# Weight rounding on one engine, the second product by groups of d_ff, contiguous decays and a shared table set in a linear attention and MLP kernel

## The chip, the cores and the metric

The kernel runs on one core of a Trainium2 chip. The time is the device time of one execution in microseconds (us), and "span" is the length of the profiled execution. TensorE (PE) multiplies, VectorE (DVE) and GpSimd (POOL) do elementwise work, ScalarE (ACT) does activations and copies, and SyncE (SP) issues most transfers. The outputs of matmuls land in PSUM, the other tiles lie in SBUF.

## The reference

Gated linear attention (4 batches, 8 heads, 768 positions, head size 48) makes 3072 rows of 384 columns. An MLP with 2048 hidden columns follows.

```python
f = 1.0 / (1.0 + np.exp(-f_logit))
for t in range(S):
    state = f[:, :, t, :, None] * state + np.einsum('bhd,bhe->bhde', k[:, :, t], v[:, :, t])
    y[:, :, t] = np.einsum('bhd,bhde->bhe', q[:, :, t], state)
x = y.transpose(0, 2, 1, 3).reshape(B * S, H * D)     # 3072 x 384
h = x @ w_in                                          # 384 x 2048
sp = np.maximum(h, 0.0) + np.log1p(np.exp(-np.abs(h)))
return ((h * erf(sp)) @ w_out).astype(np.float32)     # 2048 x 384
```

The two weights arrive as float64, since the reference scales them by a float64 number. The kernel rounds them to float32 on the chip, by arithmetic on the high and low 32-bit words.

## The kernel before

It works on 8 blocks of 384 rows, each of three token tiles (chunks) of 128. In pass `it` TensorE does the first product of block `it` in four groups of four d_ff slices, the second product of block `it - 1`, and between them the attention of block `it + 1`. There is one more pass for the last second product. A pass has 48 matmuls for each product, and the program counts them as slots, at which it inserts other engines' work.

The weights come in 16 pieces, eight for each weight, 768 columns a partition in float32. The rounding alternates between three engines:

```python
nc.scalar.activation(out=dst, in_=high.bitcast(FP32), func=AF.Abs)
yield
nc.gpsimd.tensor_scalar(out=dst, in0=dst, scalar1=TINY, scalar2=None, op0=ALU.max)
yield
nc.vector.tensor_scalar(out=bits, in0=bits, ...)              # exponent and mantissa into place
nc.vector.scalar_tensor_tensor(out=bits, in0=high, ..., in1=bits, ...)
nc.vector.tensor_scalar(out=high, in0=bits, ...)              # the mask
nc.vector.scalar_tensor_tensor(out=low, in0=low, ..., in1=high, ...)
if i >= FIRST_PIECES:
    yield
(nc.vector if i < FIRST_PIECES else nc.gpsimd).tensor_tensor(
    out=dst, in0=low.bitcast(FP32), in1=dst, op=ALU.add)
```

The second product goes by token tile. Each tile's sum has a PSUM tile of its own (of a pool of two), and needs all 16 slices of d_ff before the next tile starts:

```python
# project(it - 1, [tt], whole) for tt in 0, 1, 2
ops = {tt: ps_moe.tile([P, 2, 512], FP32, name="ops", tag="moe") for tt in tts if ...}
for ft in fts:                        # 0 .. 15
    nc.tensor.matmul(of[tt], lhsT=gr["h"][:, ft % FG, ...], rhs=w_out_sb[:, ft, :], ...)
    if ft == n_ft - 1:
        nc.scalar.copy(out=osb[:], in_=of[tt])
        nc.sync.dma_start(out=out[r : r + P, :], in_=osb[:])
```

An activation runs on a group of 1536 columns: Exp, Ln, four Squares each followed by a product on VectorE, Tanh, and a last product on VectorE. The products of the first matrix are evicted by VectorE.

## Time and profile before

The kernel took 732.22 us (median of 4 runs, 726.86 to 732.51), with a profiled span of 725.4 us.

| | PE | DVE | ACT | POOL |
|---|---|---|---|---|
| busy us before | 644.3 | 507.3 | 525.2 | 163.3 |
| share of the span | 89% | 70% | 72% | 23% |

The page's slices of the kernel before, each digit the busy share in tenths of one of 40 equal stretches (18.1 us each); PEclk is the granted clock of TensorE in tenths:

```profile
PE   2658765649799999999999999999999999999795
DVE  2788998898857765677568776679568656765640
POOL 1545877740320131001311030004202100000000
PEclk9879889779999999999999999999999999999988
```

The reader is to see two regimes: until slice 9 (about 163 us) VectorE is at least as full as TensorE; from slice 12 (about 200 us) until near the end TensorE is full. GpSimd does most of its work in the first regime.

Two further views of before: the line of TensorE's order in which the first product begins (start, duration, engine, source line, operation, in brackets the idle time before it and who ended it), and TensorE's waits after 232 us (total, times, longest):

```profile
45.88 4.40 PE L425 MATMUL hps<-xT,w_in_sb 128*128 128x384 f32 x8 [3.30 <-ACT xT L369]
...
PE ops L452 <- DVE Hg L395: 4.2, 1, 4.2
PE ops L452 <- ACT osb L460: 0.6, 1, 0.6
```

The copy of the sums (osb) costs TensorE 0.6 us in the whole of the later passes.

### The profile page before, as it was taken

What the parts mean: (1) busy time and instruction counts of PE and PEld (TensorE: products, weight loads), DVE (VectorE), ACT (ScalarE), POOL (GpSimd) and SP (SyncE); (2) the same over time, 40 slices, a digit from 0 to 9 for tenths busy, and PEclk for the clock granted to TensorE, in tenths of its full rate; (3) what the DMA queues carried; (4) which work ended last, traced back from release to release, by engine and by line L of the source; (5) the groups of instructions that cost most, each with busy time, mean ns of one, the idle gap of its engine ahead of it and who ended that gap; (6) DMA issues with size and microseconds to landing.
All of it is one profiled execution on the core that took longest, in us unless ns stands there. A gap on an engine that the chain in (4) does not pass through costs nothing.

```text
span 725.4 us, 9143 instructions
## 1 busy us (share of the span) xinstructions
PE 644.3 (89%) x3729; PEld 394.8 (54%) x3729; DVE 507.3 (70%) x422; ACT 525.2 (72%) x455; POOL 163.3 (23%) x100
## 2 busy tenths in 40 slices
PE   2658765649799999999999999999999999999795
PEld 1535442326466666666666666566666665555453
DVE  2788998898857765677568776679568656765640
ACT  4345564439898788867998599869978886889830
POOL 1545877740320131001311030004202100000000
PEclk9879889779999999999999999999999999999988
DMA  9964244600034002410223003300310000000001
GB/s 212 253 135 121 52 113 119 152 1 1 0 79 85 1 1 44 99 21 1 44 44 77 0 11 78 77 1 1 72 29 0 1 23 12 1 11 11 12 0 37
DMA packets 112176, 36.88 MB, mean 51 GB/s; under 512 B 103936, under 2 KB 107008, under 8 KB 112128
## 3 DMA queue, kind: packets, MB, share of 16 engines
q1 hardware_dynamic: 108672, 36.18, 20.9%
q8 instruction: 31, 0.51, 0.3%
q10 hardware_dynamic: 3456, 0.05, 0.2%
q14 instruction: 17, 0.14, 0.1%
HBM read 31.46 MB, written 4.72 MB: 50 GB/s over the span
## 4 chain that ended last, share of the span: by engine, by line
PE 64%; DVE 14%; ACT 11%; issue 5%; POOL 3%; DMA 2%; SPq 0%; ACTq 0%; DVEq 0%; POOLq 0%
PE ops L452 30%; PE hps L425 24%; DVE e L155 4%; PE y L144 3%; ACT x L150 2%; PE sc L323 2%; PE ps_t L310 2%; PE ps_d L279 1%; DVE Hg L248 1%; ACT e L379 1%; DVE w_out_sb L241 1%; ACT yl L382 1%; DVE w_out_sb L245 1%; DVE qd L292 1%; ACT e L393 1%
## 5 line engine op out<-in xcount | busy, mean ns | idle before, releaser
L425 PE MATMUL hps<-xT,w_in_sb 128*128 128x384 f32 x768 | 271.7, 507 | 29.4 <-DVE Hg L433 26.0
L452 PE MATMUL ops<-w_out_sb,Hg 128*128 128x384 f32 x768 | 263.2, 496 | 8.7 <-DVE Hg L395 8.2
L155 DVE SCALAR_TENSOR_TENSOR e<-x,e 128x1536 f32<-128x1536 f32 x128 | 240.1, 1876 | 6.3 <-ACT x L150 1.1
L425 PEld LDWEIGHTS hps<-xT,w_in_sb 128*128 128x128 f32 x768 | 148.1, 197 | 133.3 <-DVE Hg L433 24.2
L150 ACT ACTIVATE x<-yl,serf_bias 128x1536 f32<-128x1536 f32 x128 | 195.8, 1566 | 26.3 <-DVE e L155 25.3
L452 PEld LDWEIGHTS ops<-w_out_sb,Hg 128*128 128x128 f32 x768 | 144.8, 193 | 107.7 <-DVE Hg L395 9.4
L297 POOL TENSOR_TENSOR kd<-kn,dm 128x384 f32<-128x384 f32 x24 | 33.1, 1379 | 335.9 <-ACT dm L288 159.6
L395 DVE TENSOR_TENSOR Hg<-Hg,e 128x1536 f32<-128x1536 f32 x32 | 60.6, 1893 | 52.5 <-ACT e L393 52.3
L433 DVE COPY Hg<-hps 128x768 f32<-128x768 f32 x64 | 61.1, 955 | 35.5 <-PE hps L425 35.1
L292 DVE TENSOR_TENSOR qd<-qn,dp 128x384 f32<-128x384 f32 x24 | 23.1, 964 | 67.4 <-ACT dp L284 67.4
L393 ACT ACTIVATE e<-e 128x1536 f32<-128x1536 f32 x32 | 47.5, 1483 | 20.0 <-DVE e L155 18.4
L379 ACT ACTIVATE e<-Hg 128x1536 f32<-128x1536 f32 x32 | 47.4, 1480 | 16.0 <-DVE Hg L433 15.7
L382 ACT ACTIVATE yl<-e 128x1536 f32<-128x1536 f32 x32 | 47.5, 1484 | 0.3
L358 POOL TENSOR_TENSOR Mbd<-Sn,Tall 48x192 f32<-48x192 f32 x32 | 30.6, 956 | 61.5 <-DVE Sn L355 60.3
L144 PE MATMUL y<-A,vt 128*32 128x128 f32 x768 | 39.1, 296 | 5.8 <-DVE A L328 4.0
L382 ACT ACT_TABLE_LOAD x31 | 39.8, 1283 | 1.8 <-ACT dm L288 1.3
L144 PEld LDWEIGHTS y<-A,vt 128*32 128x32 f32 x768 | 29.7, 115 | 19.2 <-issue 11.8
L328 DVE TENSOR_TENSOR A<-sc,mask 128x1024 f32<-128x1024 f32 x24 | 29.3, 1219 | 10.2 <-PE sc L323 10.0
L284 ACT ACTIVATE dp<-ps_d 128x384 f32<-128x384 f32 x24 | 20.6, 859 | 18.0 <-PE ps_d L279 16.4
L144 PE MATMUL y<-qT,Mbd 128*32 128x128 f32 x480 | 33.1, 290 | 0.0
L323 PEld LDWEIGHTS sc<-qT,kT 48*128 48x128 f32 x384 | 23.7, 190 | 16.2 <-issue 12.5
L279 PE MATMUL ps_d<-lt,tri 128*128 128x384 f32 x48 | 21.4, 530 | 10.9 <-ACT lt L274 10.9
(59 smaller groups left out, 489.1 us busy)
## 6 DMA issues: line engine op xcount, KB each, us to landing
Hg<-in_moe_w_in_dram SPq DMA_DIRECT2D x8, 768.0 KB, 5.9
Hg<-in_moe_w_out_dram SPq DMA_DIRECT2D x8, 768.0 KB, 4.4
lt<-in_f_logit_dram SPq DMA_DIRECT2D x24, 192.0 KB, 3.7
qn<-in_q_dram SPq DMA_DIRECT2D x24, 192.0 KB, 3.8
kn<-in_k_dram SPq DMA_DIRECT2D x24, 192.0 KB, 3.6
vt<-in_v_dram SPq DMA_DIRECT2D x24, 192.0 KB, 3.7
out_dram<-osb SPq DMA_DIRECT2D x24, 192.0 KB, 2.0
Tall<-dp ACTq DMA_DIRECT2D x24, 2.0 KB, 1.9
```

The lines of the kernel that those rows point to most:

```text
L144: nc.tensor.matmul(y[M * i : M * (i + 1), kt, :], lhsT=terms[n][0], rhs=terms[n][1], start=(n == 0), stop=(n == len(terms) - 1), skip_grou ...
L150: nc.scalar.activation(out=dst[:], in_=y[:], func=AF.Square, bias=serf_bias[:, i : i + 1], scale=SERF_K)
L155: nc.vector.scalar_tensor_tensor(out=e[:], in0=x[:], scalar=SERF_AB[i][1], in1=e[:], op0=ALU.add, op1=ALU.mult)
L297: nc.gpsimd.tensor_tensor(out=kds[g % 2][:, :, 0:D], in0=kns[g % NQ][:].rearrange("t (h d) -> t h d", d=D), in1=dm[:].rearrange("t (h d) - ...
L323: nc.tensor.matmul(sc[:, r, a, :], lhsT=kT[rows(r), a, :], rhs=qT[rows(r), a, :], start=True, stop=True,)
L379: nc.scalar.activation(out=e[:], in_=h, func=AF.Exp)
L382: nc.scalar.activation(out=y[:], in_=e[:], func=AF.Ln, scale=SERF_C, bias=1.0)
L393: nc.scalar.activation(out=e[:], in_=e[:], func=AF.Tanh)
L395: nc.vector.tensor_tensor(out=h, in0=h, in1=e[:], op=ALU.mult)
L425: nc.tensor.matmul(hps[:, j, 0:TB], lhsT=w_in_sb[:, kt, ft * P : (ft + 1) * P], rhs=xTs[blk][:, kt, :], start=(kt == 0), stop=(kt == n_k - 1),
L433: nc.vector.tensor_copy(out=gr["h"][:, 2 * u : 2 * u + 2, :], in_=hps[:, :, 0:TB])
L452: nc.tensor.matmul(of[tt], lhsT=gr["h"][:, ft % FG, tt * P : (tt + 1) * P], rhs=w_out_sb[:, ft, :], start=(ft == 0), stop=(ft == n_ft - 1),)
```

## The change

The intent is to free TensorE from the rounding of the weights, which holds VectorE and GpSimd until 155 us, and to shorten the start and the tail. The main parts of the diff, cut:

```diff
@@ round_piece: all of it on VectorE, one instruction a step; words in halves of like counts
-        nc.gpsimd.tensor_scalar(out=dst, in0=dst, scalar1=TINY, scalar2=None, op0=ALU.max)
+        nc.vector.tensor_scalar(
+            out=halves(dst), in0=halves(dst), scalar1=TINY, scalar2=None, op0=ALU.max
+        )
...
-        (nc.vector if i < FIRST_PIECES else nc.gpsimd).tensor_tensor(
-            out=dst, in0=low.bitcast(FP32), in1=dst, op=ALU.add
-        )
+        nc.vector.tensor_tensor(out=dst, in0=low.bitcast(FP32), in1=dst, op=ALU.add)
@@ the raw words wait in w_out, in group buffers and in three spares
+            where = ["w", "w", "w", "w", 4, 5, 6, 3][i]
...
+            where = [4, 5, 6, "w", "w", "s0", "s1", "s2"][i - n_pieces]
@@ hidden: evictions of blocks 0 and 1 on ScalarE (and their kT copies)
+                        if blk < 2:
+                            nc.scalar.copy(out=to, in_=hps[:, :, 0:TB])
+                        else:
+                            nc.vector.tensor_copy(out=to, in_=hps[:, :, 0:TB])
@@ project: by groups of d_ff, three sums open at once in two PSUM tiles
+        ops = {tt: ps_moe.tile([P, 2, 512], FP32, name="ops", tag="moe")
+               for tt in range(0, CPB, 2)}
+        of = [ops[tt - tt % 2][:, tt % 2, 0:d_model] for tt in range(CPB)]
+        for gi in range(n_g):
+            for tt in range(CPB):
+                for j in range(FG):
...
                     if ft == n_ft - 1:
+                        osb = spares[0][:, ...]
+                        nc.scalar.copy(out=osb, in_=of[tt])
@@ one table set for Exp and Ln, loaded by hand
+    def use_exp_ln():
+        if sets[0] == EXP_LN:
+            return
+        sets[0] = EXP_LN
+        nc.scalar.add_instruction(mybir.InstLoadActFuncSet(act_func_set_id=EXP_LN, ...))
@@ stage_d: contiguous decays, their last row loaded in four parts on SyncE's queue
-        nc.scalar.dma_start(out=Tall[:, g, :], in_=dp[P - 1 : P].rearrange(...))
+        for a in range(HP):
+            nc.sync.dma_start(out=Tall[:, g, a : a + 1], in_=dp[P - 1 : P, ...])
@@ start: logits by chunk, k and v partly on ScalarE's queue
-        prepare(0, 0, CPB)
-        prepare_log(0, 0, CPB)
+        prepare(0, 0, 1)
+        prepare(0, 1, 2)
```

## The prediction

> **What bounds the kernel now.** I first read the page's forty slices: TensorE is 9 tenths busy in nearly all slices from the 12th on, at full clock, and ragged before. Then I read the busy time of each engine in four stretches, cut where TensorE's order changes: block 0's first product (46 to 120 us), the first third of the next pass (120 to 156), the rest of that pass (156 to 232) and one whole later pass (232 to 309).
>
> ```profile
> core 0: us, PE busy (x) PEld busy (x) DVE busy (x) ACT busy (x) POOL busy (x), PEclk, DMA share, GB/s
> ...
> 46.00:120.00 74.00, 55.95 (x384) 34.55 (x384) 65.76 (x59) 42.50 (x43) 49.66 (x24) 0.89 0.39 98
> 120.00:156.00 36.00, 16.37 (x58) 8.72 (x58) 32.79 (x28) 14.84 (x13) 24.81 (x11) 0.75 0.33 88
> 156.00:232.00 76.00, 71.07 (x404) 43.32 (x405) 59.65 (x46) 67.17 (x57) 11.55 (x8) 0.94 0.15 33
> 232.00:309.00 77.00, 76.42 (x469) 47.33 (x468) 51.14 (x41) 61.43 (x53) 11.91 (x8) 1.00 0.21 43
> ```
>
> From 232 us on TensorE is full; VectorE (51 of 77) and ScalarE (61 of 77) have slack. A pass is 96 matmuls, each two records of 0.3225 us (32 records took 10.32 us in the chain), 61.9 us, and about 15 us of attention: 76.8 us, which is the distance between equal places of the chain (235.2 to 312 to 389 us). Nothing in the change can shorten a full pass. What can be won lies before 232 us, where VectorE is busy 89% (65.76 of 74) and 91% (32.79 of 36) of the time, and in the tail. The waits of TensorE between 46 and 236 us name the same engine:
>
> ```profile
> PE hps L425 <- DVE Hg L433: 24.4, 4, 9.4
> PE ps_t L310 <- DVE qd L292: 6.7, 2, 6.1
> PE ps_t L310 <- DVE Sn L355: 5.6, 2, 5.3
> PE ops L452 <- DVE Hg L395: 4.0, 1, 4.0
> ```
>
> The evictions of the first product (L433) stand in VectorE's order behind the rounding of the weights. The rounding itself is stretched, as two groups of 46 to 156 us and two single instructions of the same line show:
>
> ```profile
> L241 DVE TENSOR_SCALAR w_out_sb<-w_out_sb 128x768 uint32<-128x768 uint32 x8 | 10.6, 1330 | 4.0 <-POOL w_out_sb L239 4.0
> L239 POOL TENSOR_SCALAR w_out_sb<-w_out_sb 128x768 f32<-128x768 f32 x8 | 23.7, 2974 | 0.0
> ...
> 93.88 2.22 DVE L241 TENSOR_SCALAR w_out_sb<-w_out_sb 128x768 uint32<-128x768 uint32 x1
> 105.31 0.54 DVE L241 TENSOR_SCALAR w_out_sb<-w_out_sb 128x768 uint32<-128x768 uint32 x1
> ```
>
> The same instruction took 2.22 us beside a GpSimd maximum and 0.54 us alone; its mean is 1.33 us.
>
> The tail: TensorE ran out once, for the last block's activations.
>
> ```profile
> 689.09 23.41 PE L452 MATMUL ops<-w_out_sb,Hg 128*128 128x384 f32 x64 [4.17 <-DVE Hg L395]
> ```
>
> **What the Trainium skill says.** "SBUF — State Buffer", § Who interferes with whom: a VectorE instruction in a two-port mode and a GpSimd instruction exclude each other for a whole instruction, and one with two SBUF inputs contends with GpSimd's reads. The trace agrees: 0.54 against 2.22 us. "VectorE: DVE Perf Modes", § The perf-mode tier table: in fp32 a tensor_scalar between SBUF tensors goes at 2x, a tensor_tensor at 1x; § Mode 2×_2P asks for outermost counts that are even, or equal. The trace agrees: the mask L248 takes 601 ns for w_out and 959 ns for w_in, whose two operands have unlike outer counts, and the diff's halves give them like ones. "ScalarE: Activation LUTs", § Table sets, puts Exp and Ln in one set, Tanh with Exp in another; § What ACT_TABLE_LOAD costs gives 1283 ns, which is the trace's mean, and a drain that the trace does not show (a load at 5.87 us, its activation at 7.17).
>
> **The change, part by part.**
>
> *Rounding.* Per piece, before, VectorE did four instructions for most pieces, GpSimd the maximum and the sum. Now VectorE does six. Uncontended: three at one source, 0.68 us (w_in) or 0.56 (w_out), and three with two sources at 0.96: 4.9 and 4.6 us. Sixteen pieces are 8 x 4.9 + 8 x 4.6 = 76 us, against 72 us that the before-trace's rounding groups on VectorE sum to, stretched. So VectorE takes over 74 us of GpSimd's work for 4 us of its own, and the round trips end.
>
> *Moved off VectorE.* The evictions of blocks 0 and 1, 16 x 0.95 = 15 us, and six copies of kT, 4 us, go to ScalarE (about 0.78 us for 768 columns, from 0.475 for 384 and 0.576 for 512). Onto VectorE: three kd products of block 0, 2.6 us, and six maxima of the logits, 6 x 0.77, which lie mostly later.
>
> *Start.* Logits are loaded and prepared by chunk, with the table loaded ahead: before, three loads of 1.28 us stood on the first chain, which waited to 5.9 us for all three chunks. Contiguous decays make Exp cost 0.53 us instead of 0.86. The first product started at 45.9 us; I estimate 35, as the first chunk's scan (10.9 us) may come 3 to 4 us earlier, chunks can follow each 6 us (the y of the first two stood at 22.2 and 28.5), and the third's slip to 39.6 and its copy's to 45.4 lay in waits on rounding. DMA was 93% busy until 46 us, so not much more.
>
> *First product of block 0.* In the new order VectorE has until the eighth w_in piece: six pieces 29.4, attention 3 x (0.85 + 1.22 + 0.70) + one kT and one logit maximum 1.5 = 9.8, two activation steps 3.5: 43 us. ScalarE has about 37.
>
> *To the end of rounding,* which now falls in the next pass: eight pieces 36.8, 15 activation steps and 4 products at 1.75 = 33.3, attention 8.3 + 2.2: 81 us. ScalarE in that pass: four groups x (3 x 1.48 + 4 x 1.57 + 2 x 1.28) = 53, eight evictions 6.2, seven Abs 6.4, attention 6.4, logits 3.6: 76 us. Both are near full and each waits for the other in order; in the stretch 156 to 232 the busier reached 88%. Taking 92% for the first and 90% for this: 35 + 47 + 90 = 172 us; the contiguous qd may give back some 2, so 170.
>
> *Second product by groups.* Only the last group of matmuls needs the last piece, and it is slot 72 of 96. So the pass ends at 170 + 24 x 0.645 + about 4 of attention = 189 us, against 232. Before, token tile 0 needed all sixteen slices of w_out and all four activated groups at slot 48.
>
> *Later passes* stay full. New in them: the three sums hold both PSUM tiles, so the last group's first product waits for ScalarE's copy of tile 1, issued only four matmuls (2.6 us) before; ScalarE may be two activations of 1.5 us behind. Estimate 0 to 1.5 us a pass, 4 us in all.
>
> *Tail.* The last block's fourth group is made at slots 48 to 63 instead of 72 to 83, and activation steps come each third slot: the waits of 4.2 and 1.05 us go, 5 us.
>
> Sum: 725.4 - (232 - 189) + 4 - 5 = 681 us of span; the profiled run measured 727.1 for a span of 725.4, so 682 us.
>
> **Rivals.** *TensorE full at once:* with 35 us of start, 46 for block 0's pass (48 matmuls 31 us and 15) and full passes, the second ends at 158 and the time is 650. VectorE's 124 us of sums before slot 72 speak against it. *ScalarE becomes the bound:* it gets 16 evictions, and in the second pass has 76 us against VectorE's 81; if the two alternate at 75%, rounding ends near 190 us and the time is near 702. For it: the activation chain alternates between them; against: 25 fewer table loads in the whole program order (70 against 95 before), worth 32 us of ScalarE. *The copy of the sums stalls every pass:* 3 us x 7 gives 698. Against: ScalarE idles 16 us a pass. *Start bound by DMA anyway:* the same bytes must come, so nothing is won before 46 us, and the time is 692.
>
> **Range and chances.** The rivals lie at 650, 692, 698 and 702; none of the milder ones comes back to 717 (2% below 732), and two would have to add up. Range 658 to 702. Faster 0.94, same 0.05, slower 0.01.
>
> **What would show it.** L241's counterpart should take 0.55 to 0.7 us, the mask 0.6 in both weights. First product at 35 us; VectorE busy about 90% until near 170; passes full from 189 on, 77 us apart. A wait of TensorE on ScalarE's copy of the sums beyond 1.5 us a pass, evictions late on ScalarE before 190 us, or DMA landing after its Abs is due, would make it wrong upward; VectorE ending rounding before 160 us, downward.

## The result, and the profile after

The changed kernel took 700.87 us (median of 4 runs, 698.70 to 703.94). The ratio is 0.9592 (95% interval 0.9531 to 0.9652): it is faster by 4.1%. Ratios here are the mean time of one kernel's fast runs over that of the kernel before in the same rounds, so not quite the ratio of the medians quoted. The profiled run took 698.7 us for a span of 697.0.

Source lines have moved: the first product is L476 (was L425), the second L509 (L452), the copy of the sums L518 (L460), the last product of an activation L442 (L395).

The page's slices of the kernel after (17.4 us each):

```profile
PE   3779997859999989999999989999899999999697
DVE  3779899889776675886667684675657864688410
POOL 0022101000112100011010110012001200000000
PEclk9799999989999999999999999999999999999799
```

TensorE reaches nines at the fourth slice, dips at the seventh to ninth, and is full from the tenth; GpSimd is nearly idle (66.2 us busy against 163.3). But in the right half TensorE's row has eights and a six, where before had nines and one seven, and PEclk has a seven near the end.

Windows of the kernel after, with the columns of the prediction's first fence (busy us and instructions for PE, PEld, DVE, ACT, POOL, then clock, DMA share, GB/s):

```profile
39.00:92.00 53.00, 50.14 (x388) 31.40 (x389) 46.38 (x57) 35.64 (x44) 8.83 (x8) 1.00 0.81 216
92.00:172.00 80.00, 63.99 (x353) 38.15 (x352) 71.17 (x75) 62.73 (x59) 5.36 (x5) 0.94 0.12 25
189.60:270.00 80.40, 77.61 (x467) 47.38 (x466) 51.45 (x42) 65.95 (x58) 11.04 (x7) 0.98 0.19 38
```

In the second row VectorE is busy 71.17 of 80 us, 89%, near the 90% of the prediction. The third row is one later pass, and its clock is 0.98 where the whole pass before had 1.00.

The rounding in the kernel after: one group of instructions (count, busy time, mean ns, idle before), then single ones of the mask and of GpSimd in order of time:

```profile
L270 DVE TENSOR_SCALAR w_out_sb<-w_out_sb 128x768 uint32<-128x768 uint32 x8 | 4.5, 557 | 0.1
...
41.94 0.56 DVE L279 TENSOR_SCALAR w_out_sb<-w_in_sb 128x768 uint32<-128x768 uint32 x1
50.02 1.36 DVE L279 TENSOR_SCALAR w_out_sb<-w_in_sb 128x768 uint32<-128x768 uint32 x1
...
49.60 1.36 POOL L339 TENSOR_TENSOR kd<-kn,dm 128x384 f32<-128x384 f32 x1 [4.28 <-ACT dm L329]
```

L270 is the line that took 1.33 us in the mean before. The mask, 959 ns for w_in before, took 0.56 to 0.58 us in 13 of its 16 instructions; the other three (1.25 to 1.36) ran beside a kd product on GpSimd, as the one at 50.02 does. One more line belongs to the kernel before, since the prediction reads a VectorE instruction at 105.31 us as running alone:

```profile
102.61 3.93 POOL L239 TENSOR_SCALAR w_out_sb<-w_out_sb 128x768 f32<-128x768 f32 x1
```

Three landmarks follow, from TensorE's and VectorE's order in the kernel after: the first product begins, the last piece is rounded, and the last stretch of the second pass begins.

```profile
38.98 2.85 PE L476 MATMUL hps<-xT,w_in_sb 128*128 128x384 f32 x8 [3.22 <-ACT xT L414]
...
170.47 0.96 DVE L289 TENSOR_TENSOR w_out_sb<-spare,w_out_sb 128x768 f32<-128x768 f32 x1
...
181.76 10.48 PE L476 MATMUL hps<-xT,w_in_sb 128*128 128x384 f32 x32
```

In the last line, 24 of the 32 records are the last group of that pass, the others belong to the next; so the pass ended at 181.76 + 24 x 0.3225 = 189.5 us. The same line of before stood at 224.27, which gives 232.0. The change won 42.5 us by here, and the span is shorter by only 725.4 - 697.0 = 28.4. From the end of this pass to the end of the program the kernel before took 725.4 - 232.0 = 493.4 us, and the kernel after 697.0 - 189.5 = 507.5: 14.1 us were given back in the passes that "stay full". The waits of TensorE after 189 us name where:

```profile
PE ops L509 <- ACT spare L518: 16.5, 7, 6.5
PE ps_f L559 <- DVE low L555: 1.2, 1, 1.2
```

The copy of the sums, 0.6 us before, is now 16.5 us in seven waits, one for each second product after block 0's: three of 0.57 us and four long ones. The timeline of all engines around the first of them:

```profile
252.46 0.56 ACT L356 COPY qT<-ps_t 128x512 f32<-128x512 f32 x1
...
252.93 1.57 ACT L153 ACTIVATE x<-yl,serf_bias 128x1536 f32<-128x1536 f32 x1
254.41 0.47 ACT L518 COPY spare<-ops 128x384 f32<-128x384 f32 x1
...
254.93 4.50 PE L509 MATMUL ops<-w_out_sb,Hg 128*128 128x384 f32 x8 [2.48 <-ACT spare L518]
```

TensorE stops in the midst of the second product. The eight records after the wait are four matmuls, those of token tile 1 and the last group. They wait for the copy of token tile 0, which stands in ScalarE's order behind a copy of qT and a Square. Both sums lie in one PSUM tile of two banks (the diff's `ops[tt - tt % 2][:, tt % 2, ...]`), and the wait is one between the two: a write to one bank follows the read of the other. The last three long ones:

```profile
414.77 2.85 PE L509 MATMUL ops<-w_out_sb,Hg 128*128 128x384 f32 x8 [2.92 <-ACT spare L518]
494.81 4.54 PE L509 MATMUL ops<-w_out_sb,Hg 128*128 128x384 f32 x8 [2.92 <-ACT spare L518]
...
652.84 34.13 PE L509 MATMUL ops<-w_out_sb,Hg 128*128 128x384 f32 x96 [6.47 <-ACT spare L518]
```

A wait has a second cost. At full clock the eight records take 2.85 us, as at 414.77; after two of these waits they took 4.5. The windows of the same kernel right after the first and the longest wait show the clock:

```profile
254.90:259.50 4.60, 4.58 (x14) 2.17 (x18) 3.30 (x2) 1.49 (x2) 0.00 (x0) 0.63 0.12 43
...
652.80:656.60 3.80, 3.76 (x6) 2.18 (x7) 3.59 (x3) 1.47 (x1) 0.00 (x0) 0.50 0.14 52
```

The clock is 0.63 and 0.50 of full speed, with TensorE busy all the time.

### The profile page after: what moved, and what is told of

It reads as the page before. It is cut to its first block, busy times and chain, and to the rows that moved or that the text cites. A ratio compares the mean times of both kernels' runs of the same rounds, so it can differ in the third digit from the quotient of the medians.

```text
span 697.0 us, 9216 instructions
## 1 busy us (share of the span) xinstructions
PE 637.7 (91%) x3729; PEld 389.4 (56%) x3729; DVE 474.7 (68%) x441; ACT 499.4 (72%) x456; POOL 66.2 (9%) x61
## 4 chain that ended last, share of the span: by engine, by line
PE 63%; ACT 15%; DVE 13%; issue 5%; DMA 2%; SPq 1%; POOL 0%; DVEq 0%; ACTq 0%; POOLq 0%
PE ops L509 27%; PE hps L476 24%; ACT x L153 6%; DVE e L158 6%; PE y L147 4%; PE sc L368 3%; PE ps_t L352 2%; ACT e L439 2%; PE ps_d L323 1%; DMA lt<-in_f_logit_dram 1%; ACT L439 1%; PE dS L387 1%; ACT L300 1%; ACT yl L428 1%; DVE A L373 1%
## 5 line engine op out<-in xcount | busy, mean ns | idle before, releaser
L509 PE MATMUL ops<-w_out_sb,Hg 128*128 128x384 f32 x768 | 268.6, 502 | 16.5 <-ACT spare L518 16.5
L476 PE MATMUL hps<-xT,w_in_sb 128*128 128x384 f32 x768 | 260.3, 491 | 9.8 <-ACT Hg L489 5.8
L158 DVE SCALAR_TENSOR_TENSOR e<-x,e 128x1536 f32<-128x1536 f32 x128 | 230.0, 1797 | 22.7 <-ACT x L153 18.4
L509 PEld LDWEIGHTS ops<-w_out_sb,Hg 128*128 128x128 f32 x768 | 146.0, 195 | 118.6 <-ACT spare L518 20.8
L476 PEld LDWEIGHTS hps<-xT,w_in_sb 128*128 128x128 f32 x768 | 143.6, 191 | 108.8 <-ACT Hg L489 7.6
L442 DVE TENSOR_TENSOR Hg<-Hg,e 128x1536 f32<-128x1536 f32 x32 | 56.2, 1757 | 51.3 <-ACT e L439 51.2
L491 DVE COPY Hg<-hps 128x768 f32<-128x768 f32 x48 | 45.8, 955 | 32.6 <-PE hps L476 32.4
L518 ACT COPY spare<-ops 128x384 f32<-128x384 f32 x24 | 11.3, 471 | 45.9 <-PE ops L509 45.7
L373 DVE TENSOR_TENSOR A<-sc,tri 128x1024 f32<-128x1024 f32 x24 | 29.3, 1220 | 14.3 <-PE sc L368 14.1
L147 PEld LDWEIGHTS y<-A,vt 128*32 128x32 f32 x768 | 28.4, 112 | 15.4 <-issue 9.2
L300 ACT ACT_TABLE_LOAD x27 | 34.6, 1283 | 1.3 <-PEq L911 0.8
L335 DVE TENSOR_TENSOR qd<-qn,dp 128x384 f32<-128x384 f32 x24 | 13.3, 556 | 32.2 <-ACT dp L326 32.2
L439 ACT ACT_TABLE_LOAD x27 | 34.6, 1283 | 0.5
L356 ACT COPY qT<-ps_t 128x512 f32<-128x512 f32 x24 | 13.9, 580 | 23.8 <-PE ps_t L352 23.7
```

The costliest lines, as they stand in the source:

```text
L147: nc.tensor.matmul(y[M * i : M * (i + 1), kt, :], lhsT=terms[n][0], rhs=terms[n][1], start=(n == 0), stop=(n == len(terms) - 1), skip_grou ...
L158: nc.vector.scalar_tensor_tensor(out=e[:], in0=x[:], scalar=SERF_AB[i][1], in1=e[:], op0=ALU.add, op1=ALU.mult)
L300: nc.scalar.add_instruction(mybir.InstLoadActFuncSet(act_func_set_id=EXP_LN, name=nc.get_next_instruction_name(), engine=mybir.EngineType. ...
L439: nc.scalar.activation(out=e[:], in_=e[:], func=AF.Tanh)
L442: nc.vector.tensor_tensor(out=h, in0=h, in1=e[:], op=ALU.mult)
L476: nc.tensor.matmul(hps[:, j, 0:TB], lhsT=w_in_sb[:, kt, ft * P : (ft + 1) * P], rhs=xTs[blk][:, kt, :], start=(kt == 0), stop=(kt == n_k - 1),
```

## The experiments

**Theory:** the 14 us are the copies of token tile 0, which the matmuls of tile 1 wait for because the two sums share a PSUM tile, with the slow clock after the waits. **Rivals:** ScalarE is too busy in the later passes, so that TensorE would wait for it somewhere else if not here; VectorE should have kept the copies; or the second product by groups is the wrong order for later passes, and the order by token tile belongs there. For the part that went well the question is which part of the change carries it.

All runs in one table. "Start" is the first product's start, "rounded" the end of the last piece, "pass" the end of the second pass as worked out above, "rest" the span less that; all us of the profiled run. Results were correct unless marked.

| run | start | rounded | pass | rest | median us (range) | ratio (95%) |
|---|---|---|---|---|---|---|
| before | 45.9 | 155.3 | 232.0 | 493.4 | 732.22 (726.86-732.51) | 1 |
| after | 39.0 | 171.4 | 189.5 | 507.5 | 700.87 (698.70-703.94) | 0.9592 (0.9531-0.9652) |
| e1_pair_late | 42.2 | 176.0 | 194.1 | 488.0 | 680.57 (678.90-683.88) | 0.9321 (0.9286-0.9356) |
| e2_copy_dve | 40.8 | 176.1 | 198.6 | 498.3 | 695.80 (692.77-698.67) | 0.9523 (0.9488-0.9558) |
| e3_tile_later (wrong result) | 38.0 | 173.4 | 191.6 | 492.3 | 687.56 (685.61-690.22) | 0.9413 (0.9382-0.9445) |
| e4_tile_all (wrong result) | 38.6 | 151.0 | 210.7 | 484.2 | 697.98 (696.59-701.15) | 0.9560 (0.9527-0.9592) |
| e5_round_pool | 43.9 | 200.0 | 221.8 | 488.0 | 711.37 (710.79-711.64) | 0.9727 (0.9700-0.9753) |
| e6_evict_dve | 43.4 | 184.4 | 202.5 | 487.9 | 690.74 (687.25-692.62) | 0.9433 (0.9391-0.9475) |
| e7_sets_auto | 43.4 | 182.4 | 200.5 | 489.7 | 692.40 (690.78-692.82) | 0.9466 (0.9437-0.9495) |
| e8_prep_after | 36.0 | 169.6 | 187.7 | 488.0 | 679.56 (676.25-682.91) | 0.9304 (0.9254-0.9354) |
| e9_tile_all2 | 38.0 | 150.4 | 210.4 | 488.4 | 699.66 (698.68-701.18) | 0.9578 (0.9546-0.9610) |
| e10_tall_queue | 36.8 | 174.5 | 192.6 | 488.7 | 683.58 (681.90-686.96) | 0.9369 (0.9331-0.9406) |
| e11_all | 36.7 | 173.2 | 191.3 | 485.3 | 678.52 (678.34-680.55) | 0.9299 (0.9273-0.9325) |
| e12_best | 36.0 | 169.6 | 187.7 | 483.4 | 674.55 (672.63-677.50) | 0.9237 (0.9209-0.9265) |

The kernels after, e1 to e4 and e9 have the same program until the first product, and their starts scatter from 38.0 to 42.2 us. After, e1 and e3 are the same until the sums of block 0 are copied, and scatter from 171.4 to 176.0 in "rounded" and from 189.5 to 194.1 in "pass". A difference of four or five us in these columns between two profiles is therefore not a finding; "rest" is free of it. Where two runs of different calls are compared, I take the difference of their ratios times 731 us, the time of before in those calls (730.3 to 731.5).

### e1: both copies after token tile 1

```diff
-                        osb = spares[0][:, bass.ts((blk * CPB + tt) % ..., d_model)]
-                        nc.scalar.copy(out=osb, in_=of[tt])
+                        for x in {0: (), 1: (0, 1), 2: (2,)}[tt]:
+                            osb = spares[0][:, bass.ts((blk * CPB + x) % ..., d_model)]
+                            nc.scalar.copy(out=osb, in_=of[x])
```

No work is added or removed. The copy of tile 0 is issued four matmuls later, when nothing writes the PSUM tile any more.

> Only the place of one copy in the order is changed: the sums of token tiles 0 and 1 are copied out together, after the last matmul of tile 1. Theory A (a wait for a shared buffer): tiles 0 and 1 lie in one PSUM tile, so the last matmuls of tile 1 wait for ScalarE's copy of tile 0, though they touch another bank. Then TensorE's wait of its second product on that copy goes from 16.5 us to under 1 us, the slow clock behind each wait goes too, and the time falls by 15 to 21 us to 680 to 686. Rival B (ScalarE is simply behind in the later passes): the wait moves to the next first product, which needs the same tile, and the time falls by less than 6 us.

It took 680.57 us, 20 us less than the change as it stood. The waits of TensorE on the copies in e1, after 189 us, and the pages' groups of second products in the kernel after and in e1:

```profile
PE ops L509 <- ACT spare L519: 3.2, 1, 3.2
...
L509 PE MATMUL ops<-w_out_sb,Hg 128*128 128x384 f32 x768 | 268.6, 502 | 16.5 <-ACT spare L518 16.5
...
L509 PE MATMUL ops<-w_out_sb,Hg 128*128 128x384 f32 x768 | 262.3, 494 | 3.3 <-ACT spare L519 3.2
```

Waits fell from 16.5 to 3.2 us, by 13.3. The group was busy 6.3 us less; of that 6.1 us lie in the later passes (233.8 against 227.7 us there), most of it records at slow clock. 13.3 + 6.1 = 19.4, and the rest fell from 507.5 to 488.0, by 19.5. The theory holds and accounts for all of it; the rival that ScalarE would stop TensorE elsewhere falls, since ScalarE does the same work and no other wait came. What stayed is one wait of 3.2 us in the tail. It is of another kind: the last block's first matmul takes over the PSUM tile of block 6 and waits for the pair of copies out of it.

### e2: the copies on VectorE, at once

```diff
-                        nc.scalar.copy(out=osb, in_=of[tt])
+                        nc.vector.tensor_copy(out=osb, in_=of[tt])
```

> The three copies of the sums go from ScalarE to VectorE, at their old places. A: the dependency stays, now on VectorE, which is idle 30% of a later pass but works in pieces of 1.8 us in order: a wait of 1 to 2 us in each of 8 passes stays, 8 to 15 us in all against 16.5, and the time is 692 to 702. B: ScalarE is relieved of 11 us and the time falls by as much as in the first run or more, 680 to 688.

It took 695.80 us, as expected. TensorE waited 12.5 us for VectorE's copies in eight waits, 10.2 of it after 189 us. The expectation of 1 to 2 us in each pass missed: after 189 us six waits were of 0.65 to 0.98 us, and the one in the tail was of 5.6. The other engine makes most of the waits shorter, but does not end them, and e1 with ScalarE's copies in another place is 15 us faster. It is the place of the copy that matters most here, not its engine.

### e3 and e4: the old order by token tile in the new kernel

In e3 blocks 1 to 6 go by token tile, each with a PSUM tile of its own; block 0 and the last stay by groups. In e4 block 0 goes by token tile too, and rounding is done at one step a slot throughout.

```diff
-        ops = {tt: ps_moe.tile([P, 2, 512], ...) for tt in range(0, CPB, 2)}
-        for gi in range(n_g): ... for tt in range(CPB):
+        by_tile = 0 < blk < n_blocks - 1          # e4: blk < n_blocks - 1
+        order = [(gi, tt) for tt in range(CPB) for gi in range(n_g)]     # if by_tile
+        of[tt] = ps_moe.tile([P, 2, 512], FP32, name="ops", tag="moe")[:, 0, 0:d_model]
...
-                due += 1 if it == 0 and s < 36 else 0.6     # e4 only
+                due += 1
```

> Blocks 1 to 6 have the second product by token tile again, as in the kernel before; block 0 (where the rounding ends) and the last block keep it by groups. A: each sum has its own PSUM tile again, six of the eight places of the wait go, and the time falls by 12 to 18 us, to 683 to 689, unless activations of the fourth group are due too early (then up to 697). B: no change, 697 to 704.

> Blocks 0 to 6 by token tile, and the rounding hurried to one step a slot, so that all of w_out is rounded in time. If the order by groups is what carries the gain of the start (my sum: only its last group needs the last piece, slot 72 instead of 48), the second pass ends some 15 to 20 us later than 189.6, and the time is 697 to 705, the waits saved and the start lost. If the start's gain comes from VectorE's relief alone, the second pass ends within 5 us of 189.6 and the time is 683 to 689, as in the third run.

Both gave wrong results (relative error 0.26 in e3), by a mistake of mine. The last block's fourth group is made in the midst of block 6's second product, in buffer 31 mod 7 = 3. That is the buffer of block 6's first group (24 mod 7 = 3), which by groups is done with by then, and by token tile is still to be read. The matmuls and copies are as many as in a right kernel, but what e3 and e4 show of the time is to be taken with that in mind; e9 was made to check it.

The times were as expected, 687.56 and 697.98. With separate PSUM tiles the wait for the copies was 0.6 us in each, as before the change, which agrees with e1 in another way. In e3 a new wait of 5.9 us came at 237 us, in the first pass that goes by token tile, for a group's activation (L442): by token tile all four are due by the 13th matmul of the second product.

### e9: the order by token tile with a right result

Blocks 0 to 5 go by token tile, block 6 by groups, so that the buffer is free in time; pair copies as in e1 where groups are used.

```diff
+        by_tile = blk < n_blocks - 2
...
+                        for x in {0: (), 1: (0, 1), 2: (2,)}[tt] if not by_tile else (tt,):
...
+                due += 1
```

> The fourth run mended: its result was wrong because the last block's fourth group reuses the buffer of block 6's first group, which by token tile is read until late. Here blocks 0 to 5 go by token tile, block 6 by groups with the copies of the first experiment. Expected as the fourth run did, 695 to 701 us, and correct: the order by groups is worth 14 to 20 us in the second pass.

It took 699.66 us, with a right result. Its rest is 488.4, e1's 488.0: in the later passes the two orders cost the same. The whole difference lies in the second pass. Rounding ended 21 us earlier than in the kernel after (150.4 against 171.4), and the pass ended 21 us later (210.4 against 189.5). TensorE's waits in e9 between 120 and 212 us, the two largest:

```profile
PE ops L517 <- DVE Hg L442: 13.6, 2, 12.1
PE hps L476 <- ACT Hg L489: 10.3, 1, 10.3
```

The wait of 12.1 us ended at 167.75, long after the rounding: what is missing is a group's activation. By token tile the fourth group of block 0 must be activated by the 13th of the second product's 48 matmuls, by groups only by the 37th. And the faster rounding came before those activations on VectorE: between 92 and 120 us VectorE was as busy as in e1 (26.5 against 25.8 us) but ScalarE less (17.0 against 24.5), and the evictions on ScalarE, L489, came 10.3 us late. Against e1 the order by token tile lost (0.9578 - 0.9321) x 731 = 19 us. Two limits: e9 changes the order and the pace of rounding together, since by token tile w_out must be rounded by slot 48, and no run parts the two. And with 210.4 the pass still ends 21.6 us before that of the kernel before (232.0), so half of what the change won there does not need the order by groups.

### e5: the maximum and the sum back on GpSimd (on e1)

```diff
-        nc.vector.tensor_scalar(
-            out=halves(dst), in0=halves(dst), scalar1=TINY, scalar2=None, op0=ALU.max
-        )
+        nc.gpsimd.tensor_scalar(out=dst, in0=dst, scalar1=TINY, scalar2=None, op0=ALU.max)
...
+        (nc.vector if i < 3 else nc.gpsimd).tensor_tensor(
+            out=dst, in0=low.bitcast(FP32), in1=dst, op=ALU.add
+        )
```

> On the kernel of the first experiment (e1, 680.6 us), the maximum of every piece and the sum of the fourth to sixteenth go back to GpSimd, which undoes the first part of the change in the new order. By my prediction VectorE gains and loses about as much occupancy (22 us less of its own, 24 us of stretching and waiting), and the gain of the part lies in the round trips: rounding is now one piece at a time, so each of 29 GpSimd steps of 2 to 3 us stands in VectorE's way unless other work is there. Theory: the rounding ends 10 to 25 us later, the second pass too, and the time is 690 to 706. Rival (the order matters, not the engine): within 5 us of e1, 676 to 686.

It took 711.37 us, worse than I had expected by 5 us and more: (0.9727 - 0.9321) x 731 = 30 us more than e1. VectorE's waits in e5 between 30 and 222 us:

```profile
DVE w_out_sb L268 <- POOL w_out_sb L266: 27.6, 8, 4.4
DVE w_in_sb L268 <- POOL w_in_sb L266: 27.3, 7, 5.2
```

VectorE stood 54.9 us behind GpSimd's maximum, 2.3 to 2.4 us in the mean, for an instruction that VectorE does itself in 0.56 to 0.63. (The waits also hold GpSimd's own waits for ScalarE's Abs, 21.7 us in the whole program.) In the new order pieces are rounded one at a time, while the program before had several under way; that this is why it cost more than expected is argued from the program, not shown. Of the parts taken out of e1 this one cost most.

### e6: evictions and kT copies back on VectorE (on e1)

```diff
-        if g < 2 * CPB:
+        if g < 0:
             nc.scalar.copy(out=kTs[g][:], in_=pss[1][:])
...
-                        if blk < 2:
+                        if blk < 0:
```

> On e1, the sixteen evictions of blocks 0 and 1 and the six copies of kT go back to VectorE: 19 us more for VectorE and 16 us less for ScalarE, of which some 17 us lie before the second pass ends. Theory (VectorE sets the pace to the end of rounding): that end comes 10 to 17 us later and the time is 691 to 698. Rival (the two engines alternate, so that moving work between them does not matter): 677 to 686.

It took 690.74 us, just under the 691 to 698 that were expected. Rounding ended at 184.4 instead of 176.0, later by 8.4 us and not by 10 to 17, and the pass followed it. The move is worth (0.9433 - 0.9321) x 731 = 8 us, about half of the 19 us that it takes off VectorE; with the intervals of both ratios it may be 4 to 12.

### e7: the framework's own table loads (on e1)

```diff
     def use_exp_ln():
-        if sets[0] == EXP_LN:
-            return
+        return
```

> On e1, the tables are loaded by default choice again: 101 loads instead of 70 in the whole program order, six more of 1.28 us on the way to the first product. ScalarE has 15 us a pass to spare in the later passes. Theory: only the start pays, 5 to 12 us, and the time is 686 to 693. Rival 1 (ScalarE had room everywhere): 679 to 683. Rival 2 (ScalarE's lag in the later passes matters as well): over 697.

It took 692.40 us, as expected: (0.9466 - 0.9321) x 731 = 11 us more. The trace then has 85 table loads instead of 54, and 23 instead of 8 before the end of rounding. Those of the later passes cost little, since the rest is 489.7 against 488.0; those before the end of rounding do.

Taken out of e1 one at a time, the four parts tried cost 30 us (rounding, e5), 19 (order, e9), 11 (tables, e7) and 8 (evictions, e6), 68 together, while e1 gains (1 - 0.9321) x 731 = 50 us over before. So their effects overlap, and none of these numbers is a share of the gain. The contiguous decays, the start by chunks and the new places of the raw words were taken out by no run.

### e8: block 1's logits after the last copy of xT (on e1)

```diff
+        stage_y(2)
         prepare(1, 0, CPB)
         weights_step()
-        stage_y(2)
```

The first product of the kernel after waited 3.22 us for xT. ScalarE's order there shows the reason: an Exp and a Ln of the next block's logits stood ahead of the copy.

```profile
36.20 1.16 ACT L314 ACTIVATE lt<-lt 128x1152 f32<-128x1152 f32 x1 [4.14 <-DVE lt L310]
37.40 1.16 ACT L315 ACTIVATE lt<-lt 128x1152 f32<-128x1152 f32 x1
38.47 0.46 ACT L414 COPY xT<-y 128x384 f32<-128x384 f32 x1
```

> e1, with the preparation of block 1's logits placed after the copy of block 0's last y instead of before it. In the changed kernel the first product began at 39.0 us, not the 35 that I had put, and TensorE waited 3.2 us there for that copy, which stands behind an Exp and a Ln of 1.16 us on ScalarE. Theory: the first product begins 3 to 4 us earlier, but VectorE's sums after it are unchanged, so the time falls by 1 to 4 us to 677 to 680. Rival (VectorE sets the pace anyway): within 1 us of e1.

The first product began at 36.0, and its wait for xT fell to 0.61 us. The median is 679.56, within the expected range, but only 1 us below e1 with overlapping intervals. So the start is won in the profile, while a gain in time is not shown by these rounds.

### e10: the loads of total decays on ScalarE's queue (on e8)

```diff
         for a in range(HP):
-            nc.sync.dma_start(
+            nc.scalar.dma_start(
                 out=Tall[:, g, a : a + 1],
```

On SyncE's queue the small transfers of Tall are issued among large weight pieces, and in e8 VectorE waited 3.9 us for one of them before 40 us.

> e8 with the loads of the total decays issued from ScalarE's queue instead of SyncE's, where each stands behind weight pieces of 768 KB. In the changed kernel VectorE waited 3.5 us for one of them and ScalarE 2.3 us. Theory: the first product begins 1 to 3 us earlier and the spread between runs shrinks (e1 and e8 spread over 5 and 7 us): 674 to 679. Rival (the transfers share the same engines and wait as long): as e8, 676 to 683; ScalarE issuing four small transfers a chunk could also cost it 2 us a chunk: over 683.

The theory missed, and the last rival, over 683 because issuing costs ScalarE, came true: 683.58 us, more than e8 by (0.9369 - 0.9304) x 731 = 5 us. The intervals of the two overlap; the pair e11 and e12 below, which differ in this queue alone, settles it. The wait for Tall was gone from VectorE's list before 40 us, but VectorE waited 8.4 us for the Abs of w_in pieces between 30 and 195 us, against 4.6 in e8, and rounding ended at 174.5 instead of 169.6. Issuing takes ScalarE's own time, where it is nearly full: four of these loads took 2.44 us to issue at 25.20 us, and the next copy of xT stood 2.13 us behind them.

### e11 and e12: the last block's sums in other PSUM tiles

```diff
+        if blk == n_blocks - 1:
+            two = ps_sc.tile([P, 2, 512], FP32, name="ops", tag="sc")
+            one = ps_at.tile([P, 512], FP32, name="ops1", tag="at")
+            of = [two[:, 0, 0:d_model], two[:, 1, 0:d_model], one[:, 0:d_model]]
```

The attention is over by then, and its PSUM is free; the last product needn't wait for the copies of block 6, the 3.2 us that e1 left. e11 is this on e10, e12 on e8.

> As the run before, and the last block's sums lie in the score and attention PSUM tiles, which are free by then, so that its first matmuls do not wait for the copies of block 6 (3.2 us in e1, and 2 us of slow clock behind it). Theory: 4 to 5 us below the run before, 669 to 675. Rival (the wait moves to the last block's fourth group of activations): within 1 us.

> e11 with the loads of the total decays back on SyncE's queue, that is: pair copies, preparation after the last y, the last block's sums in other tiles. The run with the other queue cost 4 us against e8 (683.6 to 679.6) in separate runs, with more waits of VectorE on ScalarE's Abs. Theory: 673 to 677. Rival (the 4 us were the spread between runs): as e11, 678 to 680.

e11 took 678.52, 5 us less than e10, as expected of the step; its level missed, since e10 was higher than foreseen. e12 took 674.55 us, as expected, with a right result. It is the best of all: 7.6% below before, and 26 us below the change as it stood. Against e11, which has only the other queue, it is (0.9299 - 0.9237) x 731 = 4.5 us faster, with intervals apart: so the queue of ScalarE does cost time. What TensorE waited for in e12 after 189 us is this, all of it, with its page's group of second products:

```profile
PE ps_f L565 <- DVE low L561: 1.2, 1, 1.2
PE ps_d L323 <- ACT lt L315: 0.3, 1, 0.3
...
L514 PE MATMUL ops<-w_out_sb,Hg 128*128 128x384 f32 x768 | 260.5, 492 | 0.0
```

## Why the prediction was right or wrong

The predicted time was 682 us, and 700.87 was measured: the sign was right, the range just held it, and the gain was 31 us where 50 were predicted. By its steps:

- **Rounding** was right. Its instructions took what was worked out (0.56 us for one source, a few above where GpSimd ran beside them; 78.1 us in all where 76 was predicted), and the old split costs 30 us in e5. The last piece was rounded at 171.4 us where 170 was predicted. One reading behind it was wrong: the 2.22 us at 93.88 stood beside GpSimd's sum (L257, 92.38 to 95.67), not a maximum, and the 0.54 us at 105.31 was not alone but within the maximum shown above (102.61 to 106.54), so these two do not compare "beside" with "alone". That work of GpSimd stretched this instruction is still so: it took 0.68 us at 33.73 and 46.13, with nothing beside it, and 1.0 to 2.3 where it began during a sum.
- **Start** was wrong by 4 us: 39.0, not 35. I had looked at the transfers and at the waits on rounding, not at what the new order puts ahead of the xT copy on ScalarE; e8 shows that, with 36.0. The error didn't reach the sum, since from the first product to the end of rounding the kernel took 132.4 us and not 135; that the two misses nearly cancel is luck.
- **Moved off VectorE** was right in its direction: e6 gives 8 us for it.
- **Second product by groups** was right: the pass ended at 189.5, predicted was 189. That it fits to 0.5 us is luck, since the same program ended this pass at 194.1 in e1's profile. e9, by token tile and with faster rounding, ends it at 210.4: some 21 of the 42.5 us hang on this order, together with the pace that it allows.
- **Later passes** is the step that failed, and it makes nearly all of the error. The prediction put it so: "the last group's first product waits for ScalarE's copy of tile 1, issued only four matmuls (2.6 us) before", with "0 to 1.5 us a pass, 4 us in all". The copy was the right suspect; which matmul waits for which copy was wrong. I had taken the buffer's reuse as the only tie. The tie that acts lies inside a buffer: the four matmuls of tile 1 write the PSUM tile that the copy of tile 0 reads, and this copy is issued right before them, with no slack in place of 2.6 us. It measured 16.5 us in seven waits, and some 6 us in slower records besides. The tie that the prediction named is real, but small: it is the 3.2 us that e1 kept in the tail, and in e10 and e11 three waits of the first product on the copies, 1.8 us in each run. The skill's page "PSUM — Partial Sum Buffer", § PSUM bank collisions raise a hardware error, tells that accesses of two engines to different banks run clean, so by the page the wait is not needed to keep the banks apart; no run has those sums in two separate tiles in the same order, so how that would do is left open (e3 and e4 had separate tiles in the other order, with 0.6 us of waits). e1 removed the wait by the order alone.
- **Tail**: the predicted 5 us were there, but hidden under the longest wait, 6.47 us, which stood in the tail. With that down to 3.2, e1's rest is 488.0, where the step says 493.4 - 5 = 488.4; and e12, without any wait on the copies, is 10 us below before, at 483.4.
- **Rivals**: "The copy of the sums stalls every pass" was the right rival, at 698 us, and was turned down with "ScalarE idles 16 us a pass". An engine that is idle a fifth of a pass can still be 2.9 or 6.5 us behind at the one moment when TensorE needs it. The mean busy share says nothing on that. "ScalarE becomes the bound" lies as near to the measured time, at 702, but it has rounding end near 190 us, and it ended at 171.4: that the times agree is chance. "Start bound by DMA" falls with the first product at 39.0 and not 46 us.

The sum with the measured terms: 725.4 - 42.5 + 14.1 = 697.0 us, where the prediction had 725.4 - 43 - 1 = 681.

## What to carry to other kernels

Where accumulators share one buffer, ask of each copy out of it which later writes go to the same buffer, and issue the copy after the last of them: here it was worth 20 us for a change of order. Take the slack of a wait from the order of issue on both engines at that place, not from the mean load of the engine. And a wait on TensorE may cost more than its length: here 13.3 us less of waits saved 19.4 us. In the kernel after, three of the four waits of 2.48 to 6.47 us were followed by slow clock, and none of the three of 0.57 us.

## What the Trainium skill lacked or had wrong

- "TensorE: Matmul & The Clock Gate", § What's actually happening, has TensorE drop to half clock after an idle window of about 3.4 us. The runs agree with the half (0.50 granted after 6.47 us of waiting), but a wait of 2.48 us was enough once (0.63 in the 4.6 us after it), of two waits of 2.92 us one was followed by slow records (4.54 us for eight) and one was not (2.85 us), and of two waits of 3.2 us at the same place one was (0.58 in the 4.0 us after it, in e1) and one was not (1.00, in e10). Another section of the page has short idles make the clock oscillate, but no length below the window is given that can do it.
- "PSUM — Partial Sum Buffer" speaks of banks and quadrants. Nothing in it warns that a program's waits may be by tile: two sums in two banks of one tile cost 16.5 us of waits, and none of this kind when they were copied as a pair (the 3.2 us left were for the next block's use of the tile).
- "ScalarE: Activation LUTs", § What ACT_TABLE_LOAD costs: the load's 1283 ns agree with the mean of 1283 ns here; the drain beside it was not seen (load at 5.87 us, next activation at 7.17 in the kernel before).
- "GPSIMD Engine Reference", § 4.1 Engine selection, advises VectorE for elementwise work but calls GpSimd's one-input operations "roughly line-rate". The maximum of 128x768 took GpSimd 2.13 us in the median of e5 (2.12 to 3.63) and VectorE 0.56 us in the kernel after, nearly four times less; spans on GpSimd are rough, but VectorE's waits of 54.9 us for it in e5 point the same way.
- "SBUF — State Buffer", § Who interferes with whom, held: the three slow masks of the kernel after (1.25 to 1.36 us against 0.56) are those beside a GpSimd product with two inputs.
